# Routing tables ahead of the first expert slot: a token table in two passes

## The chip, the cores and the metric

One core of a Trainium2 chip. The metric is device microseconds of one execution of the program. Engines are named by their work: TensorE (PE in the profile, PEld for its weight loads), VectorE (DVE), ScalarE (ACT), GpSimd (POOL), SyncE (SP, which here only issues DMAs).

## The reference, cut to what matters

Attention over 8 batches of 576 tokens gives 4608 rows x of 512 numbers. A mixture of experts follows, then a dense layer pair with a rational function. What matters here is the second stage:

```python
skip_score = x @ w_skip
do_compute = skip_score > 0
xc = x[do_compute]
logits = xc @ w_gate
e_idx = np.argmax(logits, axis=1)
...
for e in range(E):
    mask = e_idx == e
    h = np.maximum(xc[mask] @ w1[e], 0.0)
    y[mask] = gate_w[mask, None] * (h @ w2[e])
out[do_compute] = xc + y
```

There are 8 experts; w1[e] is 512 x 1024, w2[e] is 1024 x 512. Which rows belong to which expert is known only once attention is done.

## The kernel before, in words

**Stages.** `attention` writes x to the DRAM tile `xd` and keeps the logits on chip. `experts` makes routing tables, then works through up to 25 slots of 256 rows, each of one expert (a slot is two columns of 128 rows). `mlp` is the last layer pair. All matrix products are made of three passes over high and low parts in fp32r, so every weight and every x is split: ScalarE casts the high part, VectorE or GpSimd subtracts for the low part (`split`, L834).

**Routing tables** (L1019 to L1037, one hand-ordered block: inside `tc.manual_schedule()` each engine gets its instructions in the order of the text). `classify` gives one-hot experts by token; `positions` (L674) counts them on TensorE and gives each token a position, where each expert's rows start at a multiple of a slot half. `token_table` (L757) turns positions into `sidx`, the index of the token for each of 128 rows and 50 slot columns: in four parts of 12, 12, 8 and 4 token columns VectorE compares (`hh` L767 over 50 columns, `lh` L768 over 128 rows), multiplies (`tg` L769), and TensorE adds up 36 matmuls into `ptab` (L772); L776 and L777 make `sidx` of it. `slot_table` (L708) gives the expert of each slot, `etab`; it stands between the first and the second part, and behind it SP issues four loads of the first expert's w1 (L827). `kind_table` (L728) says for each slot how many of its halves hold rows (`kind`) and what the next slot needs (`change`).

**Ahead of slot 0** (L1044 to L1055, same block): `gather(0)` and `gather(1)` fetch the rows of slots 0 and 1 by indirect DMAs on GpSimd (L849), w2 comes by two loads on GpSimd (L832), w1 is split in 8 pieces, x is transposed on TensorE (L855) and split, and the last gates go to DRAM (`gate_out`).

**A slot** (L968). For slot 0 w2 is split first in 8 pieces, f odd on GpSimd (L837), and `gather_gates` (L927) fetches the gates by two indirect DMAs. Full slots run `part1_full` (L942): four groups of the first layer (`layer1` L870, 24 matmuls of 256 columns a group) each with `relu` (`hh` on ScalarE L876, `hl` on VectorE L877), then the transposes of the next slot's x, then the second layer for the slot's second half (`layer2` L886, 24 matmuls of 512 columns, in order of f), the split of the next x, and a `store` by indirect DMA on GpSimd (L894). Behind the branch come the gather of slot i + 2, the second layer for the first half and its store. In slot 0 `tables()` (L937) stands behind the four groups: `next_table` (L717), the loads of the next expert's weights, `pair_table` (L738). Outside the hand-ordered blocks the framework may put one block's instructions ahead of another's.

**Queues.** VectorE, ScalarE, GpSimd, TensorE and SP each take their instructions in order; a branch is taken by each engine for itself, with a number that it loads from a table in SBUF.

Of the kernel before, what the change touches and what calls it, by code (L numbers as in the profile page):

```python
# [19 lines left out]
E, F1 = 8, 1024  # L20
# [41 lines left out]
def tile_attention_moe_moe2(ctx: ExitStack, tc: tile.TileContext, q, k, v, w_skip, w_gate, w1, w2, w_in, w_out, ca, cb, out, dbg=None):  # L62
# [17 lines left out]
    kind = const.tile([1, 32], I32, name="kind")  # L80
    change = const.tile([1, 32], I32, name="change")
    pair = const.tile([1, 3, 32], I32, name="pair")
    early = const.tile([1, 33], I32, name="early")
# [5 lines left out]
    with ExitStack() as rst:  # L89
# [8 lines left out]
        with tc.tile_pool(name="hold", bufs=1, side="right", reuse_waits="tile") as hp:  # L98
# [6 lines left out]
            ahead, phs = [], []  # L105
            experts(tc, w1, w2, w_in, w_out, wc_in, wc_out, xd, gd, ident, logits, sidx, gates, etab, xtab, kind, change, pair, early, hold, xts, hr, wos, w2s, phs, ahead, hs, av, ab, R, dbg)
            if dbg is not None and "sidx" in dbg:
# [126 lines left out]
def attention(tc, q, k, v, w_gate, w_skip, ca, cb, ident, ones, wg, av, bv, ab, logits, xd, gd, R):  # L234
    nc = tc.nc
    with ExitStack() as st:
        inp = st.enter_context(tc.tile_pool(name="a_in", bufs=3))
        tails = st.enter_context(tc.tile_pool(name="a_tail", bufs=3))
# [211 lines left out]
        def tn(b, j):  # L450
            if j == 0:
                T["xs", b] = work.tile([P, J, DM], F32, name="xs")
            if j == J:
                T["xt", b] = work.tile([P, DM], F32, name="xt")
# [117 lines left out]
def routing_tiles(p):  # L572
    R = {}
    for name, shape, dt in (
# [3 lines left out]
            ("mx", [P, NC], F32), ("key", [P, NC], F32), ("kk", [P, NC], F32), ("gate", [P, NC], F32), ("cand", [P, NC, E], F32), ("sub", [P, NC, E], F32),  # L578
            ("onehot", [P, NC, E], BF16), ("cnt", [P, E], F32), ("eid", [1, 32], F32),
            ("pos", [P, NC], F32), ("posr", [P, NC], F32), ("rowh", [P, NH], BF16), ("rows", [1, 32], F32), ("chg", [1, 32], F32), ("nend", [1, 32], F32), ("occ", [1, NH + 2], F32), ("done", [1, 2, 64], F32), ("free", [1, 32], F32), ("posb", [P, 2, NC], BF16)):  # L580
# [92 lines left out]

def positions(tc, ps, R):  # L674
    nc = tc.nc
# [32 lines left out]
def slot_table(tc, R, etab):  # L708
    nc = tc.nc
    ends, ecmp, eid = R["cum"][0:1, 3, E:2 * E], R["cand"][0:1, 0:32, :], R["eid"]  # L710
    nc.vector.tensor_tensor(out=ecmp, in0=R["rows"].unsqueeze(2).to_broadcast([1, 32, E]), in1=ends.unsqueeze(1).to_broadcast([1, 32, E]), op=ALU.is_ge)
    nc.vector.tensor_reduce(out=eid, in_=ecmp, op=ALU.add, axis=AX.X)
    nc.vector.tensor_scalar(out=etab, in0=eid, scalar1=float(E - 1), scalar2=None, op0=ALU.min)
    nc.vector.tensor_tensor(out=R["chg"][:, 0:31], in0=eid[:, 1:32], in1=eid[:, 0:31], op=ALU.not_equal)


def next_table(tc, R, xtab):  # L717
    nc = tc.nc
    ends, ecmp, eid, nend = R["cum"][0:1, 3, E:2 * E], R["cand"][0:1, 0:32, :], R["eid"], R["nend"]
    endb = ends.unsqueeze(1).to_broadcast([1, 32, E])  # L720
# [35 lines left out]

def token_table(tc, p, ps, R, sidx):  # L757
    nc = tc.nc
    tok, posb = R["tok"], R["posb"]
    lh = p.tile([P, P, NC], BF16, name="lh")  # L760
    ptab = ps.tile([P, 2, NH], F32, name="ptab")
    c0 = 0
    for n in (CG, CG, 8, 4):
        cs = slice(c0, c0 + n)
        hh = p.tile([P, CG, NH], BF16, name="hh", bufs=2)[:, 0:n]
        tg = p.tile([P, CG, 2, NH], BF16, name="tg", bufs=2)[:, 0:n]
        nc.vector.tensor_tensor(out=hh, in0=R["rowh"].unsqueeze(1).to_broadcast([P, n, NH]), in1=posb[:, 1, cs].unsqueeze(2).to_broadcast([P, n, NH]), op=ALU.is_equal)  # L767
        nc.vector.tensor_tensor(out=lh[:, :, cs], in0=R["rowx"][:, :, 0:n], in1=posb[:, 0, cs].unsqueeze(1).to_broadcast([P, P, n]), op=ALU.is_equal)  # L768
        nc.vector.tensor_tensor(out=tg, in0=hh.unsqueeze(2).to_broadcast([P, n, 2, NH]),  # L769
                                in1=tok.rearrange("p m c -> p c m")[:, cs].unsqueeze(3).to_broadcast([P, n, 2, NH]), op=ALU.mult)  # L770
        for c in range(c0, c0 + n):
            nc.tensor.matmul(out=ptab, lhsT=lh[:, :, c], rhs=tg[:, c - c0], start=(c == 0), stop=(c == NC - 1))  # L772
        c0 += n
        yield
    high = p.tile([P, NH], F32, name="high")
    nc.vector.tensor_scalar(out=high, in0=ptab[:, 0, :], scalar1=64.0, scalar2=float(NOWHERE), op0=ALU.mult, op1=ALU.add)  # L776
    nc.vector.tensor_tensor(out=sidx, in0=high, in1=ptab[:, 1, :], op=ALU.add)  # L777
    yield


def experts(tc, w1, w2, w_in, w_out, wc_in, wc_out, xd, gd, ident, logits, sidx, gates, etab, xtab, kind, change, pair, early, hold, xts, hr, wos, w2s, phs, ahead, hs, av, ab, R, dbg=None):
    nc = tc.nc
# [4 lines left out]
    with ExitStack() as st:  # L787
# [148 lines left out]

        def tables():  # L937
            next_table(tc, R, xtab)
            load_next(0)
            pair_table(tc, R, sidx, change, pair, early)  # L940

        def part1_full(i, hh, hl):  # L942
            for f2 in range(KF // 2):
                relu(f2, layer1(i, f2), hh, hl)
            if i == 0:
                tables()
            pts = [transposes(i + 1, a) for a in range(2)] if i < MAXS - 1 else []
            py = layer2(1, hh, hl)
            for a, pt in enumerate(pts):
# [3 lines left out]
        def part1_half(i, hh, hl):  # L953
            last = i == MAXS - 1
            r = []
            for g in range(2):
                r.append(layer1_half(i, g))
            pts = []
            for g in range(2):
# [3 lines left out]
            for a, pt in enumerate(pts):  # L963
                split_x(i + 1, a, pt)
            if i == 0:
                tables()

        def slot(i, kd, ch):  # L968
            last = i == MAXS - 1
            if i == 0:  # L970
                with tc.manual_schedule():
                    for f in range(KF):
                        split_w2(f)
            with tc.manual_schedule():
                gather_gates(i)
            hh, hl = hp.tile([P, KF, SLOT], F32R, name="hh"), hp.tile([P, KF, SLOT], F32R, name="hl")
# [3 lines left out]
            with full.Else():  # L980
                with tc.manual_schedule():
                    part1_half(i, hh, hl)
            with tc.manual_schedule():
                if i + 2 < MAXS:
# [34 lines left out]
        with tc.manual_schedule():  # L1019
# [7 lines left out]
            with tc.tile_pool(name="r_ps", bufs=1, space=PSUM, reuse_waits="tile") as rps:  # L1027
                positions(tc, rps, R)
                tt = token_table(tc, rp, rps, R, sidx)
                next(tt)  # L1030
                slot_table(tc, R, etab)
                e0 = expert(etab, 0, [ET.SP, ET.Pool])
                for c in range(4):
                    load_w1(e0, c=c, n=4)
                for _ in range(4):
                    next(tt)
                kind_table(tc, R, sidx, kind, change)  # L1037
            php = hs.enter_context(tc.tile_pool(name="e_ph", bufs=1, space=PSUM, reuse_waits="tile"))
# [6 lines left out]
            for c in range(2):  # L1045
                load_w2(e0, nc.gpsimd, c, 2)
            gather(1)
            for c in range(W1A):
                split_w1(c, False)
            gate_sum(tc, R, c1, NC)  # L1050
            gate_out(tc, R, gd, (B // 2 - 1,))
            for a in range(2):
                split_x(0, a, transposes(0, a))
            for c in range(W1A, 8):
                split_w1(c, False)  # L1055
            if dbg is not None and "sidx" in dbg:
                next_table(tc, R, xtab)
# [3 lines left out]
        with tc.manual_schedule():  # L1061
            kd, ch = get(kind, 0, 2), get(change, 0, 2)
        with tc.If(kd > 0):
            slot(0, kd, ch)
        rs.close()
# [210 lines left out]
```

## Time and profile before

| what | value |
|---|---|
| runs, median (lowest to highest of 3) | 1398.18 us (1392.6 to 1401.56) |
| profiled execution, its own time | 1389.38 us |
| its span, first to last instruction | 1387.7 us |
| busy: TensorE, VectorE, ScalarE, GpSimd | 1313.0, 1106.7, 891.3, 295.3 us |
| mean granted TensorE clock | 0.977 of full speed |

Times in the rows are us from the start of the span. A row of the timeline reads: start, length, engine, line, operation, output tile <- input tiles, shapes, how many were merged, and in brackets the idle time of that engine before it with what ended it. A row of the busy times by stretch reads: stretch, its length, busy us and instructions of PE, PEld, DVE, ACT and POOL, granted clock (1.00 is 2.4 GHz), share of the DMA engines, GB/s.

### The profile page before, as it was taken

To read this page: it belongs to the slowest core of one execution; us is meant where nothing else is said; L and a number is where in the kernel's file an instruction comes from. 1 tells how busy PE (TensorE), PEld (TensorE's weight loads), DVE (VectorE), ACT (ScalarE), POOL (GpSimd) and SP (SyncE) were. 2 spreads that over 40 slices of the span, in tenths; PEclk is the share of its full clock that TensorE was granted. 3 is DMA by queue.
4 is the path that set the end of the run, shared out by engine and by line. 5 is a ranking of instruction groups with operands and counts; after the bars stand their busy time and mean duration, and the time that the engine had idled before them with its cause. 6 is when DMAs were issued, how large, how long until landed. Compare 5 with 4: busy or idle time off the path is not lost.

```text
span 1387.7 us, 22256 instructions
## 1 busy us (share of the span) xinstructions
PE 1313.0 (95%) x7470; PEld 1190.3 (86%) x7470; DVE 1106.7 (80%) x2111; ACT 891.3 (64%) x1744; POOL 295.3 (21%) x247
## 2 busy tenths in 40 slices
PE   4989489898999998799999999999999999999998
PEld 3989478877998997789999999999999999999997
DVE  6998855766747664699888888888888889898887
ACT  2656235544243432699787878787877787878786
POOL 5756044556444442241000000000000000000000
PEclk9999789999999999899999999999999999999999
DMA  9984455667555654232000000000000000000000
GB/s 278 315 279 153 130 138 200 250 210 277 216 179 207 237 204 160 82 91 69 23 24 24 24 24 24 23 24 23 24 23 24 24 24 24 24 23 24 1 23 23
DMA packets 87063, 143.90 MB, mean 104 GB/s; under 512 B 22052, under 2 KB 52772, under 8 KB 85872
## 3 DMA queue, kind: packets, MB, share of 16 engines
q1 hardware_dynamic: 79824, 125.88, 27.5%
q0 software_dynamic: 7072, 16.06, 3.7%
q8 instruction: 72, 1.18, 0.3%
q14 instruction: 95, 0.78, 0.2%
HBM read 110.66 MB, written 35.15 MB: 105 GB/s over the span
## 4 chain that ended last, share of the span: by engine, by line
PE 56%; DVE 2%; ACT 0%; issue 0%; DVEq 0%
PE py L1219 28%; PE ph L1171 28%; PE pt L1150 1%; DVE w2s L1198 0%; DVE w2s L1206 0%; DVE gl L1200 0%; DVE w2s L1208 0%; DVE w2s L1204 0%; DVE w2s L1209 0%; DVE wi0l L1128 0%; DVE w2s L1202 0%; DVE r L1202 0%; ACT w2s L1190 0%; DVE xl L1128 0%; ACT w2s L1194 0%
## 5 line engine op out<-in xcount | busy, mean ns | idle before, releaser
L1219 PE MATMUL py<-woh,gh 128*128 128x512 f32 x576 | 227.7, 395 | 0.0
L1219 PE MATMUL py<-woh,gl 128*128 128x512 f32 x576 | 226.5, 393 | 0.1
L1219 PE MATMUL py<-wol,gh 128*128 128x512 f32 x576 | 225.9, 392 | 0.0
L1180 ACT CAST gh<-w2s 128x384 fp32r<-128x384 f32 x192 | 98.6, 513 | 139.4 <-PE py L1219 131.9
L1200 DVE TENSOR_TENSOR gl<-w2s,gh 128x384 fp32r<-128x384 f32 x192 | 110.1, 573 | 65.8 <-ACT gh L1180 65.8
L1190 ACT ACTIVATE w2s<-w2s,ab 128x384 f32<-128x384 f32 x190 | 135.1, 711 | 6.3
L1219 PEld LDWEIGHTS py<-woh,gl 128*128 128x128 f32 x576 | 108.0, 188 | 24.5 <-DVE gl L1200 1.2
L1191 ACT ACTIVATE w2s<-ph,av 128x384 f32<-128x384 f32 x190 | 124.4, 655 | 0.0
L1219 PEld LDWEIGHTS py<-wol,gh 128*128 128x128 f32 x576 | 108.3, 188 | 17.0
L1219 PEld LDWEIGHTS py<-woh,gh 128*128 128x128 f32 x576 | 108.2, 188 | 17.0 <-ACT gh L1180 0.5
L1209 DVE SCALAR_TENSOR_TENSOR w2s<-w2s,av,ph 128x384 f32<-128x384 f32 x190 | 116.9, 615 | 6.7
L870 PE MATMUL ph<-xth,w1h 128*128 128x256 f32 x416 | 118.1, 284 | 0.8 <-ACT xth L835 0.7
L870 PE MATMUL ph<-xtl,w1h 128*128 128x256 f32 x416 | 117.8, 283 | 0.1
L870 PE MATMUL ph<-xth,w1l 128*128 128x256 f32 x416 | 117.6, 283 | 0.0
L1204 DVE TENSOR_TENSOR w2s<-w2s 128x384 f32<-128x384 f32 x190 | 105.7, 556 | 13.9
L1208 DVE TENSOR_TENSOR w2s<-w2s,ph 128x384 f32<-128x384 f32 x190 | 103.8, 546 | 0.0
L886 PE MATMUL py<-w2h,hl 128*128 128x512 f32 x240 | 94.8, 395 | 8.2 <-DVE hl L877 8.2
L886 PE MATMUL py<-w2h,hh 128*128 128x512 f32 x240 | 95.8, 399 | 0.0
L886 PE MATMUL py<-w2l,hh 128*128 128x512 f32 x240 | 94.4, 393 | 0.7 <-POOL w2l L837 0.7
L1189 ACT ACTIVATE w2s<-ph 128x384 f32<-128x384 f32 x190 | 92.5, 487 | 0.0
L894 POOL DMA_INDIRECT xd<-y,sidx x30 | 56.3, 1876 | 167.3 <-DVE y L893 101.3
L803 ACT ACTIVATE cvs<-raw 128x512 f32<-128x512 f32 x32 | 21.3, 677 | 107.9 <-DMA wc_in<-cvs 44.1
(268 smaller groups left out, 3510.0 us busy)
## 6 DMA issues: line engine op xcount, KB each, us to landing
hold<-in_moe_w_dram SPq DMA_DIRECT2D x8, 2048.0 KB, 8.8
w2s<-in_moe_w_dram SPq DMA_DIRECT2D x8, 2048.0 KB, 9.8
hold<-xd SPq DMA_DIRECT2D x12, 768.0 KB, 4.2
out_dram<-o SPq DMA_DIRECT2D x36, 256.0 KB, 2.2
vm<-in_v_dram SPq DMA_DIRECT2D x8, 1024.0 KB, 7.4
qm<-in_q_dram SPq DMA_DIRECT2D x8, 1024.0 KB, 11.3
xd<-xs SPq DMA_DIRECT2D x8, 1024.0 KB, 4.2
raw<-in_moe_w_in_dram SPq DMA_DIRECT2D x16, 512.0 KB, 8.1
```

Of the source, the lines that this page charges most:

```text
L870: nc.tensor.matmul(out=ph[:, u, :], lhsT=a[:, k, fs], rhs=b[:, k, :], start=(n == 0), stop=(n == 3 * KD - 1))
L886: nc.tensor.matmul(out=py, lhsT=h[:, f, ts_], rhs=w[:, f, :], start=(n == 0), stop=(n == 3 * KF - 1))
L1171: nc.tensor.matmul(out=ph, lhsT=w[:, k, :], rhs=x[k // 2][:, k % 2, :], start=(n == 0), stop=(n == 3 * KD - 1))
L1180: nc.scalar.copy(gh, pn4)
L1189: nc.scalar.activation(m, ph, AF.Abs)
L1190: nc.scalar.activation(qq, m, AF.Identity, scale=ab[:, 1:2], bias=ab[:, 0:1])
L1191: nc.scalar.activation(pn, ph, AF.Identity, scale=av[:, 3:4], bias=av[:, 2:3])
L1200: GL(nc).tensor_tensor(out=gl, in0=pn4, in1=gh.bitcast(F32), op=ALU.subtract)
L1204: nc.vector.tensor_tensor(out=qq, in0=m, in1=qq, op=ALU.mult)
L1208: nc.vector.tensor_tensor(out=pn, in0=pn, in1=ph, op=ALU.mult)
L1209: nc.vector.scalar_tensor_tensor(out=pn, in0=pn, scalar=av[:, 1:2], in1=ph, op0=ALU.add, op1=ALU.mult)
L1219: nc.tensor.matmul(out=py, lhsT=g[:, ts_], rhs=w[:, f, :], start=(f == 0 and n == 0), stop=(f == KF - 1 and n == 2))
```

## The change

`slot_table` and the loads of the first expert's w1 move into `positions`, ahead of the positions themselves. The token table is made in two passes: one over slot columns 0 and 1 (all four parts, ahead of the first gather), one over columns 2 to 49, whose first two parts follow the first gather and whose last two stand in `tables()`. `tables()` moves in a full slot 0 to behind the third group of the first layer and takes over `gather(1)`, the gates of slot 0, the w2 splits (now five of eight on GpSimd) and `kind_table`. A one-number table `kind0` decides on slot 0. The attention tiles `xs` and `xt` get a pool of their own.

```diff
 def positions(tc, ps, R, bases_done):
...
+    bases_done()
     base = cum[:, 3, E - 1:2 * E - 1]
...
-def token_table(tc, p, ps, R, sidx):
...
+CHUNKS = (CG, CG, 8, 4)
+def table_part(nc, p, R, lh, ptab, m, h0, h1):
     tok, posb = R["tok"], R["posb"]
+    nh, c0, n = h1 - h0, sum(CHUNKS[:m]), CHUNKS[m]
+    cs = slice(c0, c0 + n)
+    hh = p.tile([P, CG, nh], BF16, name=f"hh{h0}", bufs=2)[:, 0:n]
+    tg = p.tile([P, CG, 2, nh], BF16, name=f"tg{h0}", bufs=2)[:, 0:n]
+    nc.vector.tensor_tensor(out=hh, in0=R["rowh"][:, h0:h1].unsqueeze(1).to_broadcast([P, n, nh]), in1=posb[:, 1, cs].unsqueeze(2).to_broadcast([P, n, nh]), op=ALU.is_equal)
+    nc.vector.tensor_tensor(out=tg, in0=hh.unsqueeze(2).to_broadcast([P, n, 2, nh]),
+                            in1=tok.rearrange("p m c -> p c m")[:, cs].unsqueeze(3).to_broadcast([P, n, 2, nh]), op=ALU.mult)
+    if h0 == 0:
         nc.vector.tensor_tensor(out=lh[:, :, cs], in0=R["rowx"][:, :, 0:n], in1=posb[:, 0, cs].unsqueeze(1).to_broadcast([P, P, n]), op=ALU.is_equal)
+    for c in range(c0, c0 + n):
+        nc.tensor.matmul(out=ptab, lhsT=lh[:, :, c], rhs=tg[:, c - c0], start=(c == 0), stop=(c == NC - 1))
...
+def first_kind(tc, R, sidx, kind0):
+    nc = tc.nc
+    occ = R["occ"][:, 0:2]
+    nc.vector.tensor_scalar(out=occ, in0=sidx[0:1, 0:2], scalar1=float(NT), scalar2=None, op0=ALU.is_lt)
+    nc.vector.tensor_tensor(out=kind0, in0=occ[:, 0:1], in1=occ[:, 1:2], op=ALU.add)
...
         def tables():
+            for m in range(2, len(CHUNKS)):
+                table_part(nc, rest["p"], R, rest["lh"], rest["ptab"], m, 2, NH)
+            table_end(nc, rest["p"], rest["ptab"], sidx, 2, NH)
+            gather(1)
+            gather_gates(0)
+            for f in range(KF):
+                split(w2h[:, f, :], w2l[:, f, :], w2s[:, f, :], f not in (0, 2, 4))
+            kind_table(tc, R, sidx, kind, change)
             next_table(tc, R, xtab)
             load_next(0)
             pair_table(tc, R, sidx, change, pair, early)
...
             for f2 in range(KF // 2):
                 relu(f2, layer1(i, f2), hh, hl)
+                if i == 0 and f2 == 2:
+                    tables()
+            pts = [transposes(i + 1, a) for a in range(2)] if 0 < i < MAXS - 1 else []
+            py = layer2(1, hh, hl)
             if i == 0:
-                tables()
-            pts = [transposes(i + 1, a) for a in range(2)] if i < MAXS - 1 else []
-            py = layer2(1, hh, hl)
+                pts = [transposes(1, a) for a in range(2)]
...
+            if i == 0:
+                ch = get(change, 0, 2)
...
-                kind_table(tc, R, sidx, kind, change)
...
+                def first_weights():
+                    slot_table(tc, R, etab)
+                    e0.append(expert(etab, 0, [ET.SP, ET.Pool]))
+                    for c in range(4):
+                        load_w1(e0[0], c=c, n=4)
+                positions(tc, rps, R, first_weights)
+                for m in range(len(CHUNKS)):
+                    table_part(nc, rp, R, lh, ptab, m, 0, 2)
+                table_end(nc, rp, ptab, sidx, 0, 2)
+                first_kind(tc, R, sidx, kind0)
...
             gather(0)
             for c in range(2):
-                load_w2(e0, nc.gpsimd, c, 2)
-            gather(1)
-            for c in range(W1A):
+                load_w2(e0[0], nc.gpsimd, c, 2)
+            rest = dict(p=rp, lh=lh, ptab=ps["y"][0][:, 0:2 * (NH - 2)].rearrange("p (m h) -> p m h", m=2))
+            for m in range(2):
+                table_part(nc, rp, R, lh, rest["ptab"], m, 2, NH)
+            for c in range(W1A // 2):
+                split_w1(c, False)
+            for a in range(2):
+                split_x(0, a, transposes(0, a))
+            for c in range(W1A // 2, W1A):
                 split_w1(c, False)
             gate_sum(tc, R, c1, NC)
             gate_out(tc, R, gd, (B // 2 - 1,))
-            for a in range(2):
-                split_x(0, a, transposes(0, a))
```

## Rows read from the trace of the kernel before

**Rows 1.** Busy times by stretch: routing tables, last layers, two us of the first layer.

```profile
156.00:171.40 15.40, 4.78 (x43) 3.65 (x42) 13.91 (x36) 2.25 (x4) 0.00 (x1) 0.50 0.67 169
...
552.00:1387.00 835.00, 820.51 (x4172) 742.45 (x4170) 729.72 (x1404) 666.37 (x1270) 30.12 (x22) 0.99 0.09 31
...
184.00:185.00 1.00, 1.00 (x6) 1.00 (x6) 0.00 (x0) 0.00 (x0) 0.00 (x0) 0.54 0.71 270
185.00:186.00 1.00, 1.00 (x11) 1.00 (x10) 0.00 (x0) 0.00 (x0) 0.00 (x0) 1.00 1.02 414
```

**Rows 2.** Timeline of VectorE, from the positions to the first splits.

```profile
157.46 0.46 DVE L700 SCALAR_TENSOR_TENSOR r_cand<-prk,r_cum 128x288 f32<-128x288 f32 x1
...
159.48 0.78 DVE L767 TENSOR_TENSOR hh<-r_rowh,r_posb 128x600 bf16<-128x600 bf16 x1
...
162.36 0.41 DVE L711 TENSOR_TENSOR r_cand<-r_rows,r_cum 1x256 f32<-1x256 f32 x1
...
163.44 0.77 DVE L767 TENSOR_TENSOR hh<-r_rowh,r_posb 128x600 bf16<-128x600 bf16 x1
...
170.06 0.21 DVE L776 TENSOR_SCALAR high<-ptab 128x50 f32<-128x50 f32 x1 [0.58 <-PE ptab L772]
170.30 0.21 DVE L777 TENSOR_TENSOR sidx<-high,ptab 128x50 int32<-128x50 f32 x1
...
171.15 2.49 DVE L837 TENSOR_TENSOR w1l<-hold,w1h 128x512 fp32r<-128x512 f32 x4
```

**Rows 3.** Timeline of TensorE, from the transposes of x to slot 1.

```profile
177.69 1.12 PE L855 MATMUL pt<-ident,x 128*128 128x128 f32 x4 [0.91 <-DMA x<-xd,sidx]
179.48 0.58 PE L870 MATMUL ph<-xth,w1h 128*128 128x256 f32 x1 [0.67 <-ACT xth L835]
...
193.20 0.28 PE L870 MATMUL ph<-xth,w1l 128*128 128x256 f32 x1
193.31 1.04 PE L855 MATMUL pt<-ident,x 128*128 128x128 f32 x8
...
195.94 0.50 PE L886 MATMUL py<-w2l,hh 128*128 128x512 f32 x1 [0.68 <-POOL w2l L837]
...
206.05 0.28 PE L870 MATMUL ph<-xth,w1h 128*128 128x256 f32 x1
```

**Rows 4.** Timeline of GpSimd: gathers, gates and the w2 splits of slot 0.

```profile
171.40 1.53 POOL L849 DMA_INDIRECT x<-xd,sidx  x1 [32.63 <-DVE change L735]
173.23 1.28 POOL L849 DMA_INDIRECT x<-xd,sidx  x1 [0.30 <-issue]
...
189.30 1.08 POOL L930 DMA_INDIRECT gates<-gd,sidx  x1 [10.44 <-DMA gd<-r_gate]
...
193.57 1.00 POOL L849 DMA_INDIRECT x<-xd,sidx  x1 [0.30 <-issue]
194.60 5.01 POOL L837 TENSOR_TENSOR w2l<-w2s,w2h 128x512 fp32r<-128x512 f32 x4
```

**Rows 5.** Timeline of SP: the loads of the first expert's w1.

```profile
164.31 2.14 SPq L827 DMA_DIRECT2D hold<-in_moe_w_dram  x4
```

**Rows 6.** Groups by line, VectorE, 156 to 172: busy us, mean ns, idle before.

```profile
L768 DVE TENSOR_TENSOR lh<-r_rowx,r_posb 128x1536 bf16<-128x1536 bf16 (+2 forms) x4 | 3.0, 743 | 0.0
...
L733 DVE TENSOR_TENSOR kind<-r_occ 1x25 int32<-1x25 f32 x1 | 0.2, 174 | 0.0
```

**Rows 7.** Timelines of ScalarE and VectorE: `hh` and `hl` of one group, slot 1.

```profile
209.21 0.60 ACT L876 ACTIVATE hh<-ph 128x512 fp32r<-128x512 f32 x1 [13.06 <-PE ph L870]
...
209.84 0.69 DVE L877 SCALAR_TENSOR_TENSOR hl<-ph,hh 128x512 fp32r<-128x512 f32 x1 [2.84 <-ACT hh L876]
```

**Rows 8.** Timeline of VectorE: first instruction of `next_table`, and what follows `pair_table`.

```profile
196.17 3.73 DVE L721 SCALAR_TENSOR_TENSOR r_cand<-r_cand,r_cum 1x256 f32<-1x256 f32 x1
...
203.43 1.27 DVE L837 TENSOR_TENSOR xtl<-pt,xth 128x512 fp32r<-128x512 f32 x2
```

**Rows 9.** All gathers of x (L849): us from issue to landing.

```profile
DMA to landing us min/median/max: 2.1/6.8/15.2
```

More of the change, by code (lines that the diff above doesn't have):

```diff
@@ L105, in tile_attention_moe_moe2 @@
             ahead, phs = [], []
-            experts(tc, w1, w2, w_in, w_out, wc_in, wc_out, xd, gd, ident, logits, sidx, gates, etab, xtab, kind, change, pair, early, hold, xts, hr, wos, w2s, phs, ahead, hs, av, ab, R, dbg)
+            experts(tc, w1, w2, w_in, w_out, wc_in, wc_out, xd, gd, ident, logits, sidx, gates, etab, xtab, kind0, kind, change, pair, early, hold, xts, hr, wos, w2s, phs, ahead, hs, av, ab, R, dbg)
             if dbg is not None and "sidx" in dbg:
@@ L671, in gate_out, with positions @@
             nc.sync.dma_start(out=gd[r0 + i * S + MAIN:r0 + (i + 1) * S, :], in_=R["gate"][64 * i:64 * i + 64, bp * W + 2 * J:(bp + 1) * W])
-def positions(tc, ps, R):
+def positions(tc, ps, R, bases_done):
     nc = tc.nc
@@ L718, in next_table @@
     nc = tc.nc
[L719 removed]
+    ends, ecmp, eid, nend = R["cum"][0:1, 3, E:2 * E], R["ecmp"], R["eid"], R["nend"]
     endb = ends.unsqueeze(1).to_broadcast([1, 32, E])
@@ L754, in pair_table @@
     nc.vector.tensor_copy(out=pair[:, 0], in_=done[:, 1, 32:64])
-def token_table(tc, p, ps, R, sidx):
-    nc = tc.nc
[L759 to L778, printed above, removed]
@@ L781, in experts @@
-def experts(tc, w1, w2, w_in, w_out, wc_in, wc_out, xd, gd, ident, logits, sidx, gates, etab, xtab, kind, change, pair, early, hold, xts, hr, wos, w2s, phs, ahead, hs, av, ab, R, dbg=None):
+CHUNKS = (CG, CG, 8, 4)
+def table_part(nc, p, R, lh, ptab, m, h0, h1):
+    tok, posb = R["tok"], R["posb"]
+    nh, c0, n = h1 - h0, sum(CHUNKS[:m]), CHUNKS[m]
[6 more added lines that the diff above has]
+    if h0 == 0:
+        nc.vector.tensor_tensor(out=lh[:, :, cs], in0=R["rowx"][:, :, 0:n], in1=posb[:, 0, cs].unsqueeze(1).to_broadcast([P, P, n]), op=ALU.is_equal)
+    for c in range(c0, c0 + n):
+        nc.tensor.matmul(out=ptab, lhsT=lh[:, :, c], rhs=tg[:, c - c0], start=(c == 0), stop=(c == NC - 1))
@@ L782, in experts @@
+def experts(tc, w1, w2, w_in, w_out, wc_in, wc_out, xd, gd, ident, logits, sidx, gates, etab, xtab, kind0, kind, change, pair, early, hold, xts, hr, wos, w2s, phs, ahead, hs, av, ab, R, dbg=None):
     nc = tc.nc
@@ L957, in part1_half @@
                 r.append(layer1_half(i, g))
+            if i == 0:
+                tables()
             pts = []
@@ L964, in part1_half @@
                 split_x(i + 1, a, pt)
-            if i == 0:
-                tables()
         def slot(i, kd, ch):
             last = i == MAXS - 1
-            if i == 0:
+            if i > 0:
                 with tc.manual_schedule():
[L972 to L975, printed above, removed]
+                    gather_gates(i)
             hh, hl = hp.tile([P, KF, SLOT], F32R, name="hh"), hp.tile([P, KF, SLOT], F32R, name="hl")
@@ L1027, in experts @@
             with tc.tile_pool(name="r_ps", bufs=1, space=PSUM, reuse_waits="tile") as rps:
[L1028 to L1036, printed above, removed]
-                kind_table(tc, R, sidx, kind, change)
+                lh = rp.tile([P, P, NC], BF16, name="lh")
+                ptab = rps.tile([P, 2, 2], F32, name="ptab")
+                e0 = []
+                def first_weights():
[8 more added lines that the diff above has]
+                first_kind(tc, R, sidx, kind0)
             php = hs.enter_context(tc.tile_pool(name="e_ph", bufs=1, space=PSUM, reuse_waits="tile"))
@@ L1061, in experts @@
         with tc.manual_schedule():
-            kd, ch = get(kind, 0, 2), get(change, 0, 2)
+            kd = get(kind0, 0, 2)
         with tc.If(kd > 0):
-            slot(0, kd, ch)
+            slot(0, kd, None)
         rs.close()
```

16 lines of the change are left out of this document (12 added, 4 removed).

## The prediction

> **What bounds the kernel now.** The views were read from the coarse to the fine. First the busy times by stretch [rows 1]: the reader is to see that the long part behind 552 us is TensorE's (820.5 of 835 us busy), where nothing can be given back, and that the stretch from 156.00 to 171.40 is VectorE's: 13.9 of 15.4 us busy, TensorE 4.8. Between attention and the first expert slot TensorE waits for the routing tables. Then VectorE in order of time [rows 2], where one chain leads to the tokens' indices: positions from 157.46, four parts of the token table from 159.48, with the table of experts by slot (162.36 to 163.44, 1.08 us) behind the first of them, and `sidx` written at 170.30 + 0.21 = 170.51. Then TensorE and GpSimd [rows 3, 4]: the first gather starts at 171.40, 0.89 after `sidx`; when its second half has landed, x is turned at 177.69 and the first layer starts at 179.48. Every us that `sidx` comes sooner starts slot 0 a us sooner. What follows is dense on TensorE: the last first-layer matmul at 193.20, the transposes of slot 1's x at 193.31, one wait of 0.68 us, slot 1 at 206.05.
>
> The first layer has four groups of 24 matmuls, 0.11 us apart by then; the third group ended 2.7 before 193.31, at 190.6. I call that moment T. From T to the end of the first of the two runs of the second layer it took 9.9 us: that run ends 24 x 0.230 = 5.5 before 206.05, at 200.5 (0.230 is 10.11 us over the 44 matmuls from 195.94). These 9.9 us held the 8 transposes, 0.8 us.
>
> **The lead, part by part.** *First expert ahead of the positions.* The four instructions of the slot table move from 162.36 to 157.46, so the expert's number is there 4.9 us sooner, and the four w1 loads, first issued at 164.31 [rows 5], go out near 159.4. On the path of `sidx` nothing changes by this: 1.08 us stood ahead of it and still does. ScalarE has its first weights long before x, so the loads aren't what slot 0 waits for.
>
> *A pass for slot 0's two columns.* The four parts took from 159.48 to 169.48 (170.06 less the wait of 0.58), less 1.08: 8.92 us. The `lh` compares stay, 4 x 0.743 = 2.97 [rows 6]. The `hh` and `tg` of 50 columns, the other 5.95, shrink to 2 columns, at most 24 and 48 elements. The trace has none so small in bf16; the nearest row is the table operation of 25 elements at 0.174. I take eight at 0.17 = 1.36; bounds 8 x 0.10 (the like start some 0.1 apart when nothing ties them) and 8 x 0.25. So the pass takes 4.33 and `sidx` comes 8.92 - 4.33 = 4.6 us sooner (4.0 to 5.2). The wait for the last matmuls, 0.58, I leave: with 4 columns for 100 it can only be shorter, by up to 0.3.
>
> *Ahead of x.* Behind `sidx` VectorE has the two instructions of `first_kind` (0.35), then two parts of the rest of the table: 24 of 36 token columns, 48 of 50 slots, 5.95 x 0.667 x 0.96 = 3.8 us. They end 4.2 behind `sidx`, their 24 matmuls 0.5 later; x's second half was turned from 177.69, 7.2 behind it. So the transposes of x cover them; without that cover they would cost up to 4.7. The two w1 splits behind (1.25) are needed at the start of the first layer, 9.0 behind `sidx`. The new small instructions (`first_kind`, `kind` set to 0) cost nothing there. The last gate stores on SP move behind the second split of x, some 3 us later. GpSimd's read of them waited 10.4 us for their landing, to 189.30 [rows 4]; it is now asked for near 194, so this has 2 us to spare. The new T is 190.6 - 4.6 = 186.0.
>
> **What it costs behind T.** The rest of the tables now stands between the third and the fourth group, in program order on every engine.
> - TensorE's next instructions are 12 table matmuls. VectorE first does the third group's `hl`, ended 1.35 behind T (in slot 1 ScalarE started at 209.21 and VectorE ended at 210.53 [rows 7]), then `hh` and `tg` of 12 token columns: 5.95 x 0.333 x 0.96 = 1.9, to T + 3.25. The fourth group starts at T + 3.75; before, it started at T.
> - `sidx` is complete at T + 3.25 + 0.58 + 0.45 = T + 4.3 (170.06 to 170.51 for its two instructions).
> - GpSimd: the gather of slot 1 starts 0.89 later, at T + 5.2. The four indirect DMAs queued there (two gathers, two of gates) take what four took, 189.30 to 194.57 = 5.27 [rows 4]. Only then come w2's splits on GpSimd, five where there were four, at 5.01 / 4 = 1.25 each: from T + 10.45 to T + 16.7. Before, the run of four ended at 199.61, T + 9.0.
> - TensorE: the fourth group is done at T + 6.5; the second layer takes w2 in order of f and gets f = 1 from GpSimd at T + 11.7, f = 7 at T + 16.7. Its last two matmuls end at T + 17.2. The transposes of slot 1 now come behind it: T + 18.0, before 9.9. Loss 8.1.
> - VectorE beside it: three w2 splits 1.9 (2.49 for four), `kind_table` 0.6 (170.51 to 171.15), `next_table` and `pair_table` 0.4 and 3.5 (199.90 to 203.43 [rows 8]): done at T + 10.7, the last `hl` by T + 11.4, in time for f = 6.
> - `change` is now read by every engine behind the branch. It is written at T + 6.8, before TensorE gets there, and TensorE went through such reads at 206.05 without a gap: nothing, at most 0.3.
>
> **Sum.** +8.1 - 4.6 = +3.5 us. Against the profiled execution, 1389.38 (its span 1387.7 and 1.7 around it), that is 1392.9. The median of the runs shown is 8.8 above that execution; with the same 3.5 it becomes 1401.7. About 1% (14 us) is what a measurement of this kernel can tell from no change; the three runs lie between 1392.6 and 1401.56.
>
> The clock is open. TensorE worked at 1.2 GHz until 184.9, 5.4 us into the first layer: some 6 matmuls in a us beside 11 at 2.4 GHz [rows 1]. If it rises after 2 us, T is 1.7 sooner; if after 7, 0.8 later. The new waits behind T may make it fall again; the second layer is then paced by GpSimd, so a slow stretch shows only in part: 0 to +2.
>
> **A rule weighed.** While GpSimd ran its four splits, an instruction of VectorE on 256 elements with two inputs in SBUF lasted 3.73 us, from 196.17 to 199.90, where one of the same size and kind of inputs had taken 0.41 at 162.36; GpSimd's run had ended at 199.61 [rows 2, 4, 8]. The Trainium skill ("SBUF — State Buffer", Who interferes with whom) says that such an instruction contends with one of GpSimd that reads SBUF, and that the second of the two fully blocks. The trace agrees, and shows the block held over GpSimd's whole run. By the rule the tail of `pair_table` can be caught: the second rival, whose price comes from these rows.
>
> **The rivals.**
> 1. *The lead is larger than the chain (not slower).* The gathers now meet queues with less of w1's traffic, which begins 4.9 sooner. The second was turned 4.5 after it started (173.23 to 177.69 [rows 3, 4]); the shortest of the trace landed in 2.1 [rows 9]. With that, and a clock that rises after 2 us, the lead is 4.6 + 2.4 + 1.7 = 8.7 against 8.1: -0.6, 1397.6. It decides at the first layer's start: at or before 172.5 there is no loss. For it: the emptier queue. Against: w2's loads still follow at once, and the clock is luck.
> 2. *VectorE is caught by GpSimd.* `pair_table` ends at T + 10.7, GpSimd's run starts at T + 10.45. If one two-input instruction is still to come, VectorE stands until T + 16.7, the last `hl` ends at T + 17.7 and four matmuls (0.9) at T + 18.6: 1.4 more, +4.9, 1403.1. It decides at 0.3 us. For it: the row above. Against: the last four of `pair_table` have one input.
> 3. *Slot 1 starves.* Slot 2's gather was issued ahead of the branch, its second half at 193.57; now its indices aren't known there, and it stands on GpSimd behind a store of slot 0, at some T + 24. Slot 1's first layer ends at T + 18.0 + 5.5 + 4 x 2.7 = T + 34.3. A gather with the longest landing, 15.2 us [rows 9], is 5 late: +8.5, 1406.7. Against: the median is 6.8.
> 4. *No lead.* The first gather is held by something else than `sidx` (the stores of x, the weights): +8.1, 1406.3. Against: it followed `sidx` by less than a us after 33 us of idle time.
>
> **How the numbers follow.** Forecast 0.50, rival 1 0.18, rival 2 0.20, rival 3 0.07, rival 4 0.05. The likeliest gives 1401.7, on its own 1398.7 (early clock, shortest pass) to 1404.2 (clock down twice). The range reaches below to rival 1 and above to rivals 3 and 4, with part of the spread of the runs at each end: 1391 to 1409. None of the cases reaches 14 us on either side; for a cause that I don't see I leave 0.03 to faster and 0.04 to slower by over 1%, so 0.93 within.
>
> **What would show it.** Right: w1 loads issued near 159.4, slot 0's `sidx` near 165.9, the first layer near 174.9; TensorE waiting some 3.7 us for `tg` between third and fourth group, then for GpSimd's `w2l`, whose run of five starts some 10 us behind the third group; slot 1 near 209.5. Wrong: a first layer before 172.5, GpSimd's splits ahead of its gathers, or slot 1 before 206.

## The result, and the profile after

The change takes 1402.18 us in the median (1399.92 to 1408.33, 15 runs) where the kernel before takes 1393.21 (15 runs): a ratio of 1.0064, 95% interval [1.0048, 1.0081], about 9 us slower, inside the 1% that counts as no change here. The profiled execution took 1400.1 us (span 1398.4), 10.7 more than that of before. Two executions of the last experiment's kernel, of 1649 and 4619 us, are left out of its numbers.

The lead came as the forecast had it. SP's timeline has the loads of w1 where 164.31 stood [rows 5]:

```profile
159.16 2.13 SPq L837 DMA_DIRECT2D hold<-in_moe_w_dram  x4
```

VectorE's timeline, to be read beside [rows 2]: the slot table ahead of the positions, a small `hh` of the first pass, the two columns of `sidx`, and the first part of the rest of the table behind them.

```profile
157.32 0.41 DVE L714 TENSOR_TENSOR r_ecmp<-r_rows,r_cum 1x256 f32<-1x256 f32 x1
...
160.40 0.18 DVE L769 TENSOR_TENSOR hh<-r_rowh,r_posb 128x24 bf16<-128x24 bf16 x1
...
165.25 0.16 DVE L781 TENSOR_TENSOR sidx<-high,ptab 128x2 int32<-128x2 f32 x1
...
165.71 0.74 DVE L769 TENSOR_TENSOR hh<-r_rowh,r_posb 128x576 bf16<-128x576 bf16 x1
```

TensorE's timeline, to be read beside [rows 3]. The first layer starts at 173.59 instead of 179.48. Behind the last matmul of the third group stand the two waits for `tg`, the fourth group, and in the second layer a wait for GpSimd and one for VectorE; slot 1 starts at 210.91 instead of 206.05, 4.86 later.

```profile
173.59 0.58 PE L880 MATMUL ph<-xth,w1h 128*128 128x256 f32 x1 [0.67 <-ACT xth L845]
...
184.41 0.28 PE L880 MATMUL ph<-xth,w1l 128*128 128x256 f32 x1
...
187.56 0.63 PE L775 MATMUL py<-tg,lh 128*128 128x96 bf16 x8 [2.87 <-DVE tg L770]
188.42 0.46 PE L775 MATMUL py<-tg,lh 128*128 128x96 bf16 x4 [0.24 <-DVE tg L770]
188.67 0.56 PE L880 MATMUL ph<-xth,w1h 128*128 128x256 f32 x1
...
193.06 0.40 PE L896 MATMUL py<-w2h,hh 128*128 128x512 f32 x1
...
196.81 0.50 PE L896 MATMUL py<-w2l,hh 128*128 128x512 f32 x1 [2.67 <-POOL w2l L847]
...
203.53 0.50 PE L896 MATMUL py<-w2h,hl 128*128 128x512 f32 x1 [2.50 <-DVE hl L887]
...
210.91 0.28 PE L880 MATMUL ph<-xth,w1h 128*128 128x256 f32 x1
```

GpSimd's timeline (beside [rows 4]): first the gather of slot 1, in two halves; behind it the two gathers of the gates, and then the run of five splits.

```profile
190.13 1.40 POOL L859 DMA_INDIRECT x<-xd,sidx  x1 [19.12 <-DVE w2l L847]
...
195.49 6.21 POOL L847 TENSOR_TENSOR w2l<-w2s,w2h 128x512 fp32r<-128x512 f32 x5
```

VectorE beside that run. Four additions of 32 elements in `pair_table` took 7.56 us, the third of them, in the second row, 6.92 of it. That is the second rival: it ended at 201.75, as GpSimd's run did at 201.70, and the `hl` for which TensorE waits could only follow. Below, an instruction held in this way is called locked. (GpSimd's gather, which ran until 195.46, is not what held it: at 191.96 an instruction with two inputs and 256 elements took 0.41 us beside another gather.)

```profile
194.40 7.56 DVE L747 TENSOR_TENSOR r_done<-r_done 1x32 f32<-1x32 f32 x4
...
194.83 6.92 DVE L747 TENSOR_TENSOR r_done<-r_done 1x32 f32<-1x32 f32 x1
...
202.80 0.67 DVE L887 SCALAR_TENSOR_TENSOR hl<-ph,hh 128x512 fp32r<-128x512 f32 x1
```

The stretch of the fourth group, as busy time by engine with counts, then the granted clock (0.50), DMA share and GB/s: behind its wait TensorE worked at 1.2 GHz for 3.4 us.

```profile
188.50:191.90 3.40, 3.40 (x19) 3.40 (x19) 2.88 (x9) 0.97 (x2) 1.47 (x2) 0.50 0.00 0
```

Slot 0 accounts for 4.86 of the 10.7 us. The rest comes behind it, in a part of the program that the diff doesn't touch: one group of the last layers starts 8.72 us later than before, and the last run of matmuls 10.91 later (of before, then of after).

```profile
599.02 0.34 PE L1171 MATMUL ph<-xth,wi0h 128*128 128x384 f32 x1
...
1370.34 0.39 PE L1219 MATMUL py<-woh,gh 128*128 128x512 f32 x1
```

```profile
607.74 0.34 PE L1200 MATMUL ph<-xth,wi0h 128*128 128x384 f32 x1
...
1381.25 0.39 PE L1248 MATMUL py<-woh,gh 128*128 128x512 f32 x1
```

So two questions stand: what takes the lead in slot 0, and what makes TensorE slower where nothing was changed.

### The profile page after: what moved, and what is told of

It is laid out like the page before. It is cut to its first block, busy times and chain, and to the rows that moved or that the text cites. A ratio compares the mean times of both kernels' runs of the same rounds, so it can differ in the third digit from the quotient of the medians.

```text
span 1398.4 us, 22337 instructions
## 1 busy us (share of the span) xinstructions
PE 1322.2 (95%) x7506; PEld 1198.4 (86%) x7506; DVE 1111.4 (79%) x2123; ACT 891.3 (64%) x1744; POOL 297.4 (21%) x248
## 4 chain that ended last, share of the span: by engine, by line
PE 56%; DVE 2%; ACT 1%; issue 0%; DVEq 0%; ACTq 0%
PE ph L1200 27%; PE py L1248 27%; PE pt L1179 1%; DVE w2s L1227 0%; DVE gl L1229 0%; DVE w2s L1235 0%; DVE w2s L1233 0%; DVE w2s L1237 0%; DVE w2s L1231 0%; ACT gh L1209 0%; DVE wi0l L1157 0%; ACT w2s L1218 0%; ACT w2s L1219 0%; DVE w2s L1238 0%; ACT w2s L1223 0%
## 5 line engine op out<-in xcount | busy, mean ns | idle before, releaser
L1248 PEld LDWEIGHTS py<-wol,gh 128*128 128x128 f32 x576 | 108.3, 188 | 16.7
L896 PE MATMUL py<-w2h,hl 128*128 128x512 f32 x240 | 95.6, 398 | 11.0 <-DVE hl L887 10.9
```

Source lines behind the costliest of these rows:

```text
L896: nc.tensor.matmul(out=py, lhsT=h[:, f, ts_], rhs=w[:, f, :], start=(n == 0), stop=(n == 3 * KF - 1))
L1248: nc.tensor.matmul(out=py, lhsT=g[:, ts_], rhs=w[:, f, :], start=(f == 0 and n == 0), stop=(f == KF - 1 and n == 2))
```

## Experiments on slot 0

The measure is the time from the first matmul of slot 0's first layer to that of slot 1's, which leaves out when the gather came. Before: 206.05 - 179.48 = 26.57 us. Change: 210.91 - 173.59 = 37.32. So the lead is 5.89 and the loss 10.75. Four other builds told of below, whose slot 0 is that of before, took 25.24 to 27.42, and two whose slot 0 is the change's 37.05 and 37.63; a difference inside such a spread says nothing.

**Tables behind the fourth group.** `kind_table`, `next_table`, `load_next` and `pair_table` go into a function that is called behind the fourth group's relu, so that no `hl` stands behind them.

```
+        def more_tables():
             kind_table(tc, R, sidx, kind, change)
...
+            if i == 0:
+                more_tables()
```

> The change with kind_table, next_table, the next expert's loads and pair_table moved behind the relu of the fourth group, so that the last hl isn't queued behind instructions that GpSimd's splits block. If the block of VectorE (7.56 us in one instruction) costs what the trace says, TensorE then waits for GpSimd's last split alone: slot 1 near 208.6 in place of 210.9, time 2.3 us under the change. If the block is hidden behind GpSimd's own run, slot 1 stays at 210.9.

Measured: ratio 1.0093 [1.0077, 1.0109]; first layer at 176.98, slot 1 at 216.58, so 39.60 us. A miss: 2.3 worse, not better. VectorE's and TensorE's timelines:

```profile
197.82 0.69 DVE L887 SCALAR_TENSOR_TENSOR hl<-ph,hh 128x512 fp32r<-128x512 f32 x1 [2.80 <-ACT hh L886]
...
198.63 6.97 DVE L736 TENSOR_TENSOR kind<-r_occ 1x25 int32<-1x25 f32 x1
```

```profile
209.88 0.59 PE L896 MATMUL py<-w2h,hl 128*128 128x512 f32 x1 [2.21 <-DVE pair L757]
```

The `hl` is in time now, but the lock catches the first instruction with two inputs behind it, `kind`, which took 6.97 us. The tables behind it are late by that length, and the second run of the second layer waits 2.21 us for the last of them. In this order something else waits, and no less.

**All eight splits of w2 on VectorE**, on top of that.

```
-                split(w2h[:, f, :], w2l[:, f, :], w2s[:, f, :], f not in (0, 2, 4))
+                split(w2h[:, f, :], w2l[:, f, :], w2s[:, f, :], False)
```

> As the run with the tables behind, and all eight w2 splits on VectorE, none on GpSimd. If GpSimd's chain of four indirect DMAs and five splits is the rest of the loss behind the third group, the second layer runs without a wait and slot 1 starts near 205.0, 6 us under the change; what is left of the loss is the wait of 3.7 us for the late table parts. If the wait is set by something else (the gather of slot 1's x, the gates), slot 1 stays near 208.6.

Measured: ratio 1.0032 [1.0020, 1.0043]; 175.25 to 207.09, 31.84 us, 7.8 less than with the tables behind alone. With no GpSimd split on the way `kind` took 0.17 us instead of 6.97. So GpSimd's run is shown to be what holds VectorE. The 7.8 us are not the lock alone: TensorE's own waits for GpSimd's `w2l`, 2.59 and 0.27 us with the tables behind, went with it.

**`hh` and `tg` of the late parts made early.** The change with only VectorE's 2.42 us for the rest's last two parts moved ahead of slot 0; the twelve matmuls, the splits and the tables stay.

```
-            for m in range(2, len(CHUNKS)):
-                table_part(nc, rest["p"], R, rest["lh"], rest["ptab"], m, 2, NH)
+            for add_up in rest["late"]:
+                add_up()
...
+            rest["late"] = [table_part(nc, rp, R, lh, rest["ptab"], m, 2, NH) for m in range(2, len(CHUNKS))]
```

> The change with one thing moved: hh and tg of the rest's last two parts (2.42 us of VectorE) are made before slot 0, beside their first two parts; their twelve table matmuls stay behind the third group, and so do the splits and the tables. Theory (two losses in a row, the wait for tg and then the lock by GpSimd's run): the sums don't wait, TensorE is not idle there for 2.87 us, sidx and gather(2) and with them the GpSimd run and the end of the lock all come 2.5 to 3.3 us sooner behind the third group; the run of five still locks VectorE for 6 to 8 us, and slot 1 starts 2.5 to 3.3 us sooner behind the end of the third group than in the change (there 26.2 us). Ratio 1.003 to 1.005. Rival (the wait for tg is only one of several parallel ones, and the lock's end is set by w2's casts or landing): slot 1 less than 1 us sooner.

Measured: 177.04 to 211.43, 34.39 us, 2.9 less than the change: in the range. The sums follow the third group at once, and the lock is there as before:

```profile
187.70 0.28 PE L883 MATMUL ph<-xth,w1l 128*128 128x256 f32 x1
187.82 0.93 PE L777 MATMUL py<-tg,lh 128*128 128x96 bf16 x12
```

```profile
194.92 7.54 DVE L747 TENSOR_TENSOR r_done<-r_done 1x32 f32<-1x32 f32 x4
```

The whole time did not show it: ratio 1.0068 [1.0046, 1.0090], where 1.003 to 1.005 was expected. In the profiled execution x was late, and the first layer began 3.4 us later than in the change's. How much of that stands in the other executions was not separated.

**Both waits taken away.** `hh` and `tg` early, the twelve matmuls behind the second group, all eight splits on VectorE in the gaps between groups, the tables behind the fourth, and `kind0` in a spare column of `change` (why is told in the next section).

```
-                relu(f2, layer1(i, f2), hh, hl)
+                ph = layer1(i, f2)
+                if i == 0 and f2 == 1:
+                    table_sums()
+                relu(f2, ph, hh, hl)
+                if i == 0 and f2 == 0:
+                    split_w2s(0, 1, 2)
+                if i == 0 and f2 == 1:
+                    table_rest()
+                    split_w2s(3, 4, 5)
                 if i == 0 and f2 == 2:
-                    tables()
+                    split_w2s(6, 7)
```

> Keeps the change's own table pass, but takes both new waits of slot 0 away: hh and tg of the rest's last two parts are made before slot 0, their twelve table matmuls stand behind the second first-layer group, all eight splits of w2 run on VectorE in the gaps between the groups (three, three, two), and the four later tables stand behind the fourth group; the first expert's number lies in a spare column of another tile, so that the weight tiles stand at the same place within 128 bytes as in the kernel before. Theory (the change lost its lead to the wait for tg and to the GpSimd run that holds VectorE): no wait between third and fourth group, no lock, slot 1 starts 4 to 7 us before that of the kernel before, whole time 0.994 to 0.997 of before. Rival (the lead can't be had, something else binds slot 0, such as w2's landing or gather(2)): slot 1 starts no more than 1 us earlier, ratio 0.999 to 1.003.

Measured: 1387.6 us (1387.04 to 1388.96, 6 runs), ratio 0.9941 [0.9919, 0.9962]: faster than both. The timeline of TensorE from slot 0 to slot 1 has no wait between these rows; 25.99 us.

```profile
175.50 0.58 PE L883 MATMUL ph<-xth,w1h 128*128 128x256 f32 x1 [0.68 <-ACT xth L848]
...
183.41 0.93 PE L777 MATMUL py<-tg,lh 128*128 128x96 bf16 x12
...
201.49 0.28 PE L883 MATMUL ph<-xth,w1h 128*128 128x256 f32 x1
```

Slot 1 starts 4.56 us sooner than before: 3.98 are the lead, and the other 0.58 lie inside the spread of slot 0. Of that the end keeps 2.3 (span 1385.4): 2.9 are given back in slot 3. There a run of four GpSimd splits locks VectorE again, as in the kernel before; TensorE waits 4.96 us for the `hl` behind it (before 3.65), and then works at 1.2 GHz for 3.3 us, which it doesn't before. The medians differ by 8.7 us; what the other executions have beyond those 2.3 us, no trace shows. Timelines of VectorE, GpSimd and TensorE, and the stretch behind the wait:

```profile
248.53 6.07 DVE L850 TENSOR_TENSOR w2l<-w2s,w2h 128x512 fp32r<-128x512 f32 x1 [0.35 <-ACT w2h L848]
...
249.10 4.95 POOL L850 TENSOR_TENSOR w2l<-w2s,w2h 128x512 fp32r<-128x512 f32 x4
...
255.26 0.80 PE L899 MATMUL py<-w2h,hl 128*128 128x512 f32 x1 [4.96 <-DVE hl L890]
```

```profile
255.10:258.40 3.30, 3.14 (x7) 2.48 (x8) 3.09 (x6) 1.84 (x4) 2.42 (x3) 0.50 0.61 150
```

**The kernel before with the splits on VectorE**, to see whether these alone bring it: in slot 0's loop `split_w2(f)` becomes the split with `False`.

> The kernel before with all eight splits of slot 0's second weights on VectorE. It tells whether the gain of the version that beats both comes from the splits alone. Theory (that gain is the change's lead, kept): slot 0 of before has only one wait of 0.68 us in its second layer, so slot 1 starts between 0.7 us sooner and 0.5 us later, ratio 0.998 to 1.001. Rival (the splits alone do it): slot 1 starts 3 to 5 us sooner, ratio 0.994 to 0.997.

Measured: ratio 0.9993 [0.9973, 1.0012], 179.01 to 204.80, 25.79 us. 25.79 lies among the 25.24 to 27.42 of builds with the splits left where they were, so the splits alone win nothing that can be seen, in slot 0 or in the whole time. What the trace of the faster version has ahead of the kernel before at slot 1 is the change's lead, kept.

## Experiments on the pace behind slot 0

The change adds two tiles ahead of the weights: `kind0` (32 bytes as placed) and `r_ecmp` (32 x 8 x 4 = 1024). Tiles placed behind both stand 1056 bytes further, those behind the first alone 32: in either case 32 more, counted within 128. (These places are worked out from the sizes of the tiles; no row shows an address.) The first idea was that the start within 64 bytes sets the matmuls' pace, so that 32 bytes more would restore it and 32 bytes in the kernel before would spoil it.

```
+    pad = const.tile([1, 8], I32, name="pad")
+    nc.gpsimd.memset(pad, 0)
```

> The change with 32 bytes of unused table ahead of all tiles of the left side of SBUF, so that the weights stand again at an odd multiple of 32 bytes, as before the change. Theory 1 (two causes: slot 0 is 4.9 us late, and the matmuls that read x from the held tiles became some 2 ns slower because the weights moved by an odd multiple of 32 bytes): slot 1 still starts near 210.9, but first-layer matmuls come 117.5 ns apart again in place of 119.5, those of the last layers on the held x 173.6 in place of 176.2, and the time is 3 to 5 us under that of the change, near 1.0035 of the kernel before. Rival (all of it comes from slot 0 and from where the clock happened to fall): paces and time stay, 1.0064.

> The kernel before with the same 32 bytes added and nothing else. Theory 1: slot 1 starts at 206.1 as before, first-layer matmuls come 119.5 ns apart, the held-x ones of the last layers 176, and the time is 3 to 5 us over that of the kernel before, ratio 1.002 to 1.0035. Rival (slot 0 alone): paces 117.5 and 173.6, ratio 1.000.

Measured: the padded change 1.0138 [1.0118, 1.0157], the padded kernel before 1.0047 [1.0032, 1.0062]. The padded kernel before became slower, as the idea has it, and by more than the 1.002 to 1.0035 expected. The padded change contradicts it: another 32 bytes made it worse, not good. So the place within 128 bytes was tried: 64 bytes of pad before, 32 bytes less before (`qc` as a third column of `ab`), and the change with `kind0` in a spare column of `change`, which leaves 1024.

```
-    kind0 = const.tile([1, 1], I32, name="kind0")
+    kind0 = change[:, 31:32]
```

> The kernel before with 64 bytes of unused tile among its constants: nothing moves but the places of the tiles behind them. Theory (place within 128 bytes): as in the padded change, a first layer of an expert slot takes 11.51 us instead of 11.30, the offset grows by 4.5 us between 590 us and the end, whole time 7 to 9 us over before, ratio 1.005 to 1.0065. Rival 1 (only the place within 64 bytes counts, which is that of before): ratio 1.000. Rival 2 (run to run only): ratio within 0.0015 of 1.000 and the first layer at 11.30.

> The kernel before with one 32-byte constant tile laid into another: the tiles behind stand 32 bytes earlier, the fourth of the four places within 128 bytes. Theory (each place has its own pace, in the order 32 fastest, 64, 96): the fourth is either the fastest yet or the slowest, which the three others don't tell; between 0.997 and 1.009. Rival (only 64 bytes count): the pace of the kernel with 32 bytes more, 11.39 us for a first layer and ratio 1.0025 to 1.0045.

> The change with its one new constant tile (32 bytes, the first expert's number) laid into a spare column of an existing one. The weight tiles then stand 1024 bytes further than before instead of 1056, at the same place within 128 bytes. Theory (the place of the weights sets the pace of the matmuls): a 96-matmul first layer of an expert slot takes 11.30 us as before (11.40 in the change), the offset to before no longer grows between 590 us and the end (2.1 in the change), and the ratio falls by 0.0025 to about 1.004. Rival (the pace comes from elsewhere, such as when loads run): 11.40 and the growth stay, ratio 1.006.

Measured ratios: 1.0026 [1.0007, 1.0045], 1.0020 [0.9998, 1.0041] and 1.0049 [1.0033, 1.0066]. The first misses its 1.005 to 1.0065, and the last can't be told from the change's 1.0064. TensorE's timelines show what the times don't. The first matmul of one expert slot, the first transposes behind its 96 matmuls, and the two marks of the last layers, first for 64 bytes more, then for the change with `kind0` folded:

```profile
374.97 0.28 PE L872 MATMUL ph<-xth,w1h 128*128 128x256 f32 x1
...
386.49 0.27 PE L857 MATMUL pt<-ident,x 128*128 128x128 f32 x1
...
603.66 0.33 PE L1173 MATMUL ph<-xth,wi0h 128*128 128x384 f32 x1
...
1379.44 0.39 PE L1221 MATMUL py<-woh,gh 128*128 128x512 f32 x1
```

```profile
384.61 0.28 PE L880 MATMUL ph<-xth,w1h 128*128 128x256 f32 x1
...
395.92 0.27 PE L865 MATMUL pt<-ident,x 128*128 128x128 f32 x1
...
612.06 0.34 PE L1200 MATMUL ph<-xth,wi0h 128*128 128x384 f32 x1
...
1383.40 0.39 PE L1248 MATMUL py<-woh,gh 128*128 128x512 f32 x1
```

The same two differences in every kernel of the study:

| place within 128 bytes, against before | kernels | first layer of that slot | mark to mark in the last layers |
|---|---|---|---|
| same | before, change folded, memset alone, splits alone, version without waits | 11.30 to 11.31 | 771.31 to 771.34 |
| 32 more | change, padded before, tables behind, splits on VectorE, `tg` early, version without waits and unfolded | 11.39 to 11.40 | 773.46 to 773.51 |
| 64 more | padded change, before with 64 | 11.51 to 11.52 | 775.76 to 775.78 |
| 32 less | before with 32 less | 11.36 | 775.71 |

No idle time separates them; the matmuls follow each other at another distance, and fourteen kernels fall on four values. A kernel that also alters slot 0 falls with the others of its place. (A few first layers of a kernel, beside waits or a change of clock, took longer or shorter; the table has the undisturbed ones.) So the pace is shown to come from the place of the tiles, and it costs the change 773.51 - 771.32 = 2.2 us behind the mark and 0.08 in each full first layer, 0.9 over the eleven from slot 2 on: about 3.

As a control, the kernel before with one memset more and nothing moved:

> The kernel before with one more GpSimd memset of a 32-element tile at its start and no tile moved: what the padded kernels have beside their shift. Theory (the shift costs, not the instruction): ratio within 0.0015 of 1.000, a first layer of an expert slot 11.30 us, no growth of the offset behind 590 us. Rival (any new build of the kernel differs by as much as the padded ones did): a ratio of 1.002 or more.

Measured: ratio 1.0003 [0.9982, 1.0024], pace as before. What the places make of the whole time is less sure: the median of before was 1391.3 to 1396.3 from one set of runs to another, and the 64 bytes came to 3.6 us of the 7 to 9 expected, though their profiled execution was 9.2 longer. The steadiest pair is the version without waits, run once more with `kind0` as its own tile:

> The version without waits in slot 0, now with the change's own 32-byte tile for the first expert's number, so that the weight tiles stand 32 bytes further within 128 bytes than in its other build; the instructions are the same. That build ran within 1387.0 and 1389.0 us, so some 3 us show here better than beside the kernel before. Theory (place of the weights): a first layer of an expert slot takes 11.40 us instead of 11.31, the last stage grows by 2.1 us, median 1390 to 1392.5. Rival (the place costs nothing in a whole run): median 1387 to 1389.

Measured: ratio 1.0004 [0.9981, 1.0027], 1388.1 to 1397.4 us in the executions compared (their median, 1393.3, lies above the 1390 to 1392.5 expected), where the folded one lay within 1387.0 and 1389.0. Of two builds with the same instructions one beats before and the other doesn't. The profiled execution of the second started slot 1 2.59 us sooner than the first's (198.90) and still ended 1.1 later. The pace accounts for some 3 us of that; the rest of what lies between the two ratios isn't explained, and they come from two sets of runs, each against its own executions of before.

## Why the prediction was right or wrong

*The time.* 1401.7 was forecast and 1402.18 measured, but the agreement is partly that of the base: the forecast took +3.5 onto a median of three runs, 1398.18; fifteen put it at 1393.21. The difference itself is 9.0, and 3.5 was too small. (The ends given for the likeliest case alone, 1398.7 and 1404.2, don't follow from its terms: an early clock, the shortest pass and the shortest wait, 1.7 + 0.6 + 0.3, lead to 1399.1. Nothing else is built on them.)

*The lead.* Mechanism right. The w1 loads went out at 159.16 (159.4 forecast), `sidx` was written at 165.41 (165.9), the first layer began at 173.59 (174.9). The pass took 4.2 us (4.33), its eight small operations 1.4 together (1.36). Of the 1.3 beyond the 4.6, 0.5 are `sidx` itself and 0.8 lie between the first gather and the first layer (7.30 us for 8.08), which rival 1 had named. But this execution was a lucky one: the seven other kernels that have the change's lead began slot 0 at 172.83 to 177.04, in the middle at 175.50. A lead of 4 is typical. In two of them, those with `kind0` folded, the indices came later, at 166.69 and 167.16. In four the gather started 2.3 to 3.4 us behind its indices instead of 0.9; for three of these four the DMA issues show what came late. In the padded change the store of x's rows to DRAM landed after 11.3 us,

```profile
xd<-xs SPq DMA_DIRECT2D x1, 1024.0 KB, 11.3
```

where it was 7.3 before and 9.2 in the profiled change. (With the tables behind and with the splits on VectorE it was 10.9.) The first gather, which reads these rows, then started at 168.41. With w1's loads 5 us earlier the store shares the queues with them. That need not be all of it: in all four executions SP's row of two gate stores ahead of these loads was already 3.6 to 4.2 us long, where the change's was 1.1. Why, stays open.

*The loss behind T.* Forecast 8.1, measured 10.9 (slot 0 as a whole lost 10.75, since the clock rose sooner). The wait for `tg` was right: the fourth group at T + 4.1 (3.75; T is 184.53, 0.12 behind the last start of the third group). `hh` and `tg` of the two late parts took 2.4 us for 1.9, and with them `sidx` and GpSimd came 0.5 late: the run at T + 11.0 (10.45), its end at T + 17.2 (16.7). The step that failed is "VectorE done at T + 10.7, the last `hl` by T + 11.4, in time". The third of the four additions started at T + 10.3, 0.66 us ahead of GpSimd's first split, and was held until T + 17.2; the last `hl` ended at T + 18.9 and the run of matmuls at T + 20.0 instead of 17.2. These 2.8 us are the second rival (1.4), GpSimd's later start (0.5), 0.7 for the rest of `pair_table`, which kept the `hl` until 202.80 and for most of which that rival had no term, and 0.2 in the last four matmuls. Its sum, +4.9, met the 4.86 at slot 1 by two errors that cancel: a lead 1.3 larger, a loss 1.3 larger. The forecast's reason against it, that the last four of `pair_table` have one input, was true and beside the point: they weren't reached. Nor did "it decides at 0.3 us" hold, since an instruction whose record begins 0.66 ahead of the run's was caught.

*The clock.* It rose at 178.3, 4.7 into the first layer, and fell for the 3.4 us shown above. That delayed the fourth group to T + 8.5 (6.5), but behind it everything waited for GpSimd: it cost nothing at slot 1, as "shows only in part" had it.

*Rivals 3 and 4.* Slot 1 did not starve; its successor started without a gap. A lead there was.

*What no step named.* The pace, about 3 us, by two tiles whose place nobody would have called a cost. And between slot 1 and the last layers some 3 us more, net, of which three pieces are seen. In slot 3, which took 1.5 longer, the clock fell again behind a wait, which it didn't before (the first stretch is of the change, the second of before; each begins 0.22 behind the start of the matmul that ended the wait).

```profile
263.60:267.10 3.50, 3.50 (x9) 2.74 (x9) 2.71 (x5) 2.18 (x4) 2.73 (x3) 0.51 0.68 199
```

```profile
258.65:262.15 3.50, 3.50 (x16) 2.89 (x16) 2.72 (x5) 2.18 (x4) 2.13 (x3) 1.00 0.75 221
```

Nine matmuls stand there for sixteen. The wait itself was 3.49 us in the change and 3.65 before, so its length doesn't tell the two apart; why the clock falls there in the change and in the version without waits, and not before, stays open. From one later full slot to the next, 325.94 to 357.41, the change took 1.6 longer (before 320.04 to 349.94). And ahead of the first group of the last layers TensorE waited 6.53 us instead of 4.97 (of the change, then of before):

```profile
579.34 0.66 PE L1200 MATMUL ph<-xth,wih 128*128 128x384 f32 x1 [6.53 <-DVEq L1111]
```

```profile
570.57 0.61 PE L1171 MATMUL ph<-xth,wih 128*128 128x384 f32 x1 [4.97 <-DVEq L1082]
```

Some of this is won back in between. From the first matmul of slot 1 to that of L1171 (before 206.05 to 570.57, 364.5 us) kernels of the same place took 364.3 to 371.1, so this part of the 9 us is the least explained.

## What to carry to other kernels

Before work is put late on VectorE, look for every run of GpSimd elementwise instructions that can meet it: here such a run held a VectorE instruction with two inputs in SBUF from the run's first record to its last, and what waited behind was late by the run and by the rest of the queue. A lead that ends in a wait is worth nothing until the waits are taken away one by one, in the order in which they end last; here the same lead came with +9 us, and without the waits with -8 in one build and nothing in the other. And when a diff adds a tile, compare the distance of matmuls in a stage that the diff does not touch: a shift of 32 bytes moved it by 0.3 to 0.7%.

## What the runs showed that was not expected

- GpSimd's hold on VectorE covers a run of five back-to-back instructions without a gap, 6.92 us for an addition of 32 elements, and takes an instruction whose record begins 0.66 us ahead of the run's first. The Trainium skill ("SBUF — State Buffer", Who interferes with whom) has the engine that issues first hold the shared ports for the whole of its instruction; the runs show the hold over five instructions, and the records of the starts don't tell which engine issued first. In the Trainium skill "Perfetto Trace Analysis" (GPSIMD Engine Instruction) puts the recorded start of a GpSimd instruction that reads at its first read, behind steps that the record doesn't show. That would fit the 0.66; no run here measures these steps.
- The pace of matmuls depends on the place of their tiles within 128 bytes: 11.31, 11.36, 11.39 and 11.52 us for the same 96 matmuls, the same in every kernel of one place. The order is not the same in both stages (32 less is second in the first layer and nearly last in the last layers). Which of the operands' places counts was not tried.
